# Preparing the second layer's weight sums in other pieces, on other engines and queues, while the first layer runs

## The chip, the cores and the metric

One core of a Trainium2 chip runs the whole kernel. TensorE (PE) multiplies matrices, with its weight loads recorded apart as PEld; VectorE (DVE), ScalarE (ACT) and GpSimd (POOL) do the element work, and SyncE (SP) issues DMAs and nothing else. ACT issues DMAs too. Every engine takes its instructions strictly in the order in which they were written, so an instruction that waits holds up all that stands behind it on its engine. The metric is the time of one execution on the device in microseconds: before the change the median of three runs is 1815.99 us (1813.62 to 1821.92).

## The reference

Three stages follow one another on 8 sequences of 576 tokens with 512 features.

```python
# 1: attention inside chunks of 64 tokens, 8 heads of 64
attn = softmax(q_c @ k_c^T / sqrt(64));  x = attn @ v_c
# 2: first layer
xn = (x - mean) / sqrt(var + 1e-6) * g_ln
x  = x + relu(xn @ w_ch1) @ w_ch2            # 512 -> 2048 -> 512
# 3: second layer, with its own weights
u   = x + (x^T @ U @ V)^T                     # U 576x32, V 32x576: mixes tokens
out = u + relu(u @ w_ch1') @ w_ch2'           # 512 -> 2048 -> 512
```

The weights, U and V arrive as 64-bit floats, which the kernel takes as pairs of 32-bit words and converts itself.

## The kernel before

Every matmul runs on operands split into a high and a low part, three products for one. The 4608 tokens are 36 tiles of 128.

**First layer.** Twelve blocks of three tiles, 16 steps each, 192 steps in all. A step is `g1` (12 matmuls of 384 columns into `psh`), then ScalarE's relu (L659, high part) and VectorE's L660 (low part), and `g2` of the step two back (9 matmuls of 512 columns into `acc`). At the end of a block `finish` (L677) adds `acc` onto `x` on VectorE, three tiles, and the next block's accumulation can begin only then. All else is written in between: the attention of a later block (L361/362 transposes, small matmuls into `psm`, L460 to L479 softmax on VectorE, L469 exp on ScalarE, scattered to DRAM as `sp` by ScalarE's queue at L586 and gathered at L591, L485 transpose, L514 the scaled result), its layer norm (L520 to L544), another scatter and gather, and L596, L598, L599 on VectorE, ScalarE and GpSimd, which give the next block's input. `z_mm` and `z_out` (L622) form the rank-32 product for the low-rank term and put it out as `zd`.

**Weights of the second layer.** The second layer uses a seven-product (Strassen-like) scheme on 256-wide halves, so it wants block sums of its weights. They are made beside the first layer, in 16 units, the first weight's eight before the second's. A unit loads two raw pieces of 512 KB (ScalarE's queue, L174 or L176), scales the two words of each on ScalarE (L186, L187), joins them on VectorE in a burst of five instructions (L192, L193, L196, L197, L198: `pre_b`), forms four sums on GpSimd (L219 to L222, 128x256 each: `pre_s`), splits seven results in a high part (ScalarE's L231) and a low part (VectorE's L236), and stores each result (256 KB, ScalarE's queue, L241, `wd<-wsp`), through two output slots in turn. A step is cut into thirds, and `at3` puts every piece of unit u into third 160 + 22u + x, with x from a table; steps 53 to 173.

**Second layer.** Five superblocks of 7, 7, 8, 7, 7 tiles, 112 units of six matmuls each (448 or 512 columns). Its weights come back from `wd` by 560 loads of 256 KB on SP (`w_in`, L962) into a ring. At a superblock's end the results are transposed by VectorE (L946, into four buffers `zt`) and stored (L957, `out<-zt`, four DMAs a tile), while the next superblock's tokens are loaded from `x1d` (L770, four DMAs a tile), turned by VectorE (L777) and given the low-rank term: `zd` is loaded on all partitions (L631), summed on GpSimd (L635), rounded (L642, L643), multiplied (`pslow`) and added by VectorE (L805). All three loads and the stores share SP's queue. `l2_first` writes this for the first superblock into the last 16 steps of the first layer, from step e = 176.

```python
at(NF * (NB - 2) + 13, make_vst)                       # V converted in step 173
for u in range(2 * NPR):                               # block sums: u-th unit
    for x, fn, n in ((0, pre_load, 0), (9, pre_load, 1), (5, pre_a, 0), (8, pre_b, 0), ...
        at3(160 + 22 * u + x, fn, u, ...)
```

Of the kernel before, what the change touches and what calls it, by code (L numbers as in the profile page):

```python
# [18 lines left out]
def fused_kernel(ctx, tc, q, k, v, g_ln, w1_a, w2_a, U, V, w1_b, w2_b, out):  # L19
    nc = tc.nc  # L20
# [12 lines left out]
    SB = (7, 7, 8, 7, 7)  # L33
    NPR = NF // 2
# [38 lines left out]
    w_d = {(w, m, p): dr.tile([P, DM], F32, name=f"wd{w}_{m}_{p}") for w in range(2) for m in range(7) for p in range(NPR)}  # L73
# [95 lines left out]
    def pre_load(u, n):  # L169
        which, p = divmod(u, NPR)  # L170
        f = 2 * p + n
        raw = pre[u, n] = raw_tile()
        if which:
            nc.scalar.dma_start(out=raw.rearrange("p a w -> p (a w)"), in_=w2_b.bitcast(I32)[f * P:(f + 1) * P, :])  # L174
        else:
            nc.scalar.dma_start(  # L176
                out=raw.rearrange("p (k f) w -> p k (f w)", k=KT),
                in_=w1_b.bitcast(I32)[:, f * 2 * P:(f + 1) * 2 * P].rearrange("(p k) f -> p k f", k=KT),
            )

    def pre_words(u, n):
        return pre[u, n][:, :, 1], pre[u, n][:, :, 0]

    def pre_a(u, n):
        hw, lw = pre_words(u, n)
        nc.scalar.activation(out=hw.bitcast(F32), in_=hw.bitcast(F32), func=AF.Copy, scale=2.0 ** -112)  # L186
        nc.scalar.activation(out=lw.bitcast(F32), in_=lw.bitcast(U32), func=AF.Copy, scale=2.0 ** -52)  # L187

    def pre_b(u, n):
        e = pl["e"]  # L190
        hw, lw = pre_words(u, n)
        nc.vector.tensor_scalar(out=e.bitcast(I32), in0=hw, scalar1=0x0FFFFFFF, scalar2=3, op0=ALU.bitwise_and, op1=ALU.logical_shift_left)  # L192
        nc.vector.scalar_tensor_tensor(out=hw, in0=hw, scalar=-0x80000000, in1=e.bitcast(I32), op0=ALU.bitwise_and, op1=ALU.bitwise_or)  # L193

        hw, lw = (a.bitcast(F32) for a in (hw, lw))
        nc.vector.tensor_scalar(out=e.bitcast(I32), in0=hw.bitcast(I32), scalar1=-0x00800000, scalar2=None, op0=ALU.bitwise_and)  # L196
        nc.vector.tensor_tensor(out=lw, in0=lw, in1=e, op=ALU.mult)  # L197
        nc.vector.tensor_tensor(out=hw, in0=hw, in1=lw, op=ALU.add)  # L198

    def pre_blocks(u):  # L200
        which = u // NPR
        e, z = [], []
        for n in range(2):
            hw, lw = (a.bitcast(F32) for a in pre_words(u, n))
            if which == 0:
                v = hw.rearrange("p (t c) -> p t c", t=KT)
            else:
                v = hw.rearrange("p (c t) -> p t c", t=KT)
            e.append([v[:, 0:2], v[:, 2:4]])
            z += [lw[:, m * 256:(m + 1) * 256].rearrange("p (t c) -> p t c", t=2) for m in range(2)]  # L210
        (a11, a12), (a21, a22) = e
        if which:
            a12, a21 = a21, a12
        return a11, a12, a21, a22, z

    def pre_s(u):
        a11, a12, a21, a22, (s1, s2, s3, s4) = pre_blocks(u)
        tt = nc.gpsimd.tensor_tensor
        tt(out=s1, in0=a21, in1=a22, op=ALU.add)  # L219
        tt(out=s2, in0=s1, in1=a11, op=ALU.subtract)  # L220
# [12 lines left out]

    def pre_l(u, c):
        m, o, x = pre["c", c]
        nc.vector.tensor_tensor(out=o[:, 1], in0=x, in1=f32(o[:, 0]), op=ALU.subtract)  # L236

    def pre_d(u, c):
        which, p = divmod(u, NPR)
        m, o, x = pre["c", c]  # L240
        nc.scalar.dma_start(out=w_d[which, m, p], in_=f32(o).rearrange("p w t c -> p (w t c)"))  # L241
# [347 lines left out]
    def gather(key):  # L589
        w = t1.tile([P, 4, P], F32, tag="w" if key < 2 * NT else "cvd", name="w")  # L590
# [29 lines left out]
    def z_out(b):  # L620
        z4 = t1.tile([P, DM], F32, tag="xn" if b >= B - 2 else "cvd", name="z4")
# [61 lines left out]
    O = (0, 1, 5, 6, 4, 2, 3)  # L683
    UNITS = 2 * 7 * NPR
# [647 lines left out]
```

## Time and profile before

| quantity | value |
|---|---|
| median of three runs | 1815.99 us (1813.62 to 1821.92) |
| the profiled execution | 1820.96 us |
| its span | 1819.1 us |
| PE busy | 1672.3 us, 92% of the span |
| VectorE busy | 1156.7 us, 64% |
| ScalarE busy | 601.8 us, 33% |
| GpSimd busy | 353.4 us, 19% |
| mean granted TensorE clock | 0.969 |

The profiled execution is 5 us above the median and within the three runs. Times of rows count from the start of the span; the first layer's steps with block sums beside them run from about 330 to 936 us, its last 16 steps to 1030 us, the second layer after them. [...]

### The profile page before, as it was taken

The page shows a single profiled execution, that of the slowest core. Times are in us where ns is not written, and L with a number is a line of the kernel's source. Part 1 is how long each engine was busy: PE and PEld are TensorE (multiplying, and loading weights), DVE is VectorE, ACT ScalarE, POOL GpSimd, SP SyncE. Part 2 cuts the span into 40 slices and gives each one's busy share as a digit, 9 for nine tenths or more (in the row PEclk, how much of TensorE's full clock was granted, in tenths as well). Part 3 has the DMA queues.
Part 4 walks back from the last instruction along what each step waited for, and adds up shares of the span by engine and source line. Part 5 has one row for each costly group of instructions (what it writes and reads, how often), then busy time and mean ns, then how long its engine had stood idle before and what let it go on. Part 6 is the DMA issues. An engine that isn't in the chain of part 4 may idle for free.

```text
span 1819.1 us, 28472 instructions
## 1 busy us (share of the span) xinstructions
PE 1672.3 (92%) x9890; PEld 1454.7 (80%) x9890; DVE 1156.7 (64%) x2384; ACT 601.8 (33%) x1122; POOL 353.4 (19%) x355
## 2 busy tenths in 40 slices
PE   6899998989899999999989999989997999899995
PEld 5788887878788788778777898978986888799994
DVE  7887544564756667576644259638836963884774
ACT  5554211222222232233221233424432442344341
POOL 1000011212122122212130033132033205202410
PEclk8999999999999999999989999999998999899998
DMA  6443333556466574556424288778776766777772
GB/s 163 125 131 100 93 72 77 147 144 170 136 160 169 154 197 145 151 165 166 144 91 149 84 243 256 214 200 259 207 200 205 237 192 195 244 226 215 251 214 77
DMA packets 384431, 307.94 MB, mean 169 GB/s; under 512 B 196513, under 2 KB 277409, under 8 KB 384290
## 3 DMA queue, kind: packets, MB, share of 16 engines
q1 hardware_dynamic: 314602, 230.22, 45.7%
q10 hardware_dynamic: 69688, 75.92, 13.3%
q8 instruction: 79, 1.29, 0.3%
q14 instruction: 62, 0.51, 0.1%
HBM read 241.53 MB, written 64.49 MB: 168 GB/s over the span
## 4 chain that ended last, share of the span: by engine, by line
PE 42%; DMA 10%; DVE 5%; issue 3%; SPq 2%; POOL 2%; ACT 1%; ACTq 1%; DVEq 0%; POOLq 0%
PE ps L60 31%; PE acc L60 5%; PE psh L60 4%; DMA out<-zt 3%; DMA zr<-zd 3%; DMA wr<-wd 2%; SPq L957 1%; DMA xw<-x1d 1%; DMA sp<-xn 1%; DVE zt L946 1%; DMA w<-sp 1%; PE psm L60 0%; PE pslow L60 0%; POOL zr L635 0%; ACTq L586 0%
## 5 line engine op out<-in xcount | busy, mean ns | idle before, releaser
L60 PE MATMUL ps<-act,wr 128*128 128x448 f32 (+1 forms) x2100 | 465.0, 379 | 12.9 <-POOL act L833 5.6
L60 PEld LDWEIGHTS ps<-act,wr 128*128 128x128 f32 x2100 | 402.1, 193 | 62.5 <-POOL act L833 6.4
L60 PE MATMUL psh<-act,w0h 128*128 128x384 f32 x1536 | 407.2, 346 | 41.5 <-DVE act L660 20.1
L60 PE MATMUL acc<-w1h,act 128*128 128x512 f32 x1152 | 403.2, 404 | 12.6 <-ACT e L469 9.6
L60 PEld LDWEIGHTS psh<-act,w0h 128*128 128x128 f32 x1536 | 287.6, 193 | 69.8 <-DVE act L660 28.0
L60 PEld LDWEIGHTS acc<-w1h,act 128*128 128x128 f32 x1152 | 219.6, 191 | 65.9 <-ACT e L469 11.0
L60 PE MATMUL psh<-act,w0l 128*128 128x384 f32 x768 | 263.9, 344 | 0.9 <-DVE w0l L148 0.9
L660 DVE SCALAR_TENSOR_TENSOR act<-psh,act 128x384 fp32r<-128x384 f32 x192 | 106.1, 553 | 243.3 <-ACT act L659 243.1
L60 PE MATMUL acc<-w1l,act 128*128 128x512 f32 x576 | 229.7, 399 | 0.0
L659 ACT ACTIVATE act<-psh 128x384 fp32r<-128x384 f32 x192 | 93.9, 489 | 298.4 <-PE psh L60 198.2
L60 PEld LDWEIGHTS psh<-act,w0l 128*128 128x128 f32 x768 | 148.0, 193 | 1.2 <-DVE w0l L148 1.2
L60 PEld LDWEIGHTS acc<-w1l,act 128*128 128x128 f32 x576 | 110.1, 191 | 17.9
L231 ACT CAST wsp<-raw 128x256 fp32r<-128x256 f32 x112 | 53.7, 480 | 180.0 <-DMA wd<-wsp 42.0
L890 ACT ACTIVATE h<-h 128x448 f32<-128x448 f32 (+1 forms) x80 | 46.8, 591 | 143.2 <-DVE h L900 101.5
L524 POOL TENSOR_SCALAR rs<-mv 128x1 f32<-128x1 f32 x36 | 8.4, 234 | 432.0 <-DVE mv L522 424.2
L236 DVE TENSOR_TENSOR wsp<-raw,wsp 128x256 fp32r<-128x256 f32 x112 | 61.2, 547 | 29.6 <-ACT wsp L231 25.3
L599 POOL TENSOR_TENSOR act<-wT,act 128x512 fp32r<-128x512 f32 x27 | 34.8, 1287 | 195.8 <-ACT act L598 187.0
L896 DVE TENSOR_TENSOR h<-ps,h 128x448 f32<-128x448 f32 (+1 forms) x40 | 24.1, 626 | 70.2 <-PE ps L60 70.2
L635 POOL TENSOR_TENSOR zr<-zr 128x512 f32<-128x512 f32 x24 | 30.9, 1287 | 189.3 <-DMA zr<-zd 183.6
L883 POOL TENSOR_TENSOR h<-h,h 128x448 f32<-128x448 f32 (+1 forms) x40 | 52.5, 1330 | 42.8 <-DVE hr0l L870 21.5
L929 POOL TENSOR_TENSOR uq<-rs,uq 128x448 f32<-128x448 f32 (+1 forms) x9 | 11.8, 1334 | 189.2 <-DVE uq L923 145.9
L60 PE MATMUL ps<-hr0h,wr 128*128 128x448 f32 (+1 forms) x140 | 47.0, 375 | 0.3 <-issue 0.2
(222 smaller groups left out, 2558.2 us busy)
## 6 DMA issues: line engine op xcount, KB each, us to landing
wr<-wd SPq DMA_DIRECT2D x560, 256.0 KB
wd<-wsp ACTq DMA_DIRECT2D x112, 256.0 KB
raw<-in_moe_w_ch ACTq DMA_DIRECT2D x32, 512.0 KB
w<-sp ACTq DMA_DIRECT2D x54, 256.0 KB
x1d<-x SPq DMA_DIRECT2D x36, 256.0 KB
xw<-x1d SPq DMA_DIRECT2D x144, 64.0 KB
v_pl<-in_v SPq DMA_DIRECT2D x132, 64.0 KB
raw<-in_moe_w_ch SPq DMA_DIRECT2D x64, 128.0 KB
```

The source lines that it names most:

```text
L60: nc.tensor.matmul(o, lhsT=l, rhs=r, start=start, stop=stop, **kw)
L231: nc.scalar.copy(out=o[:, 0], in_=src[m])
L236: nc.vector.tensor_tensor(out=o[:, 1], in0=x, in1=f32(o[:, 0]), op=ALU.subtract)
L599: nc.gpsimd.tensor_tensor(out=lo, in0=x, in1=f32(hi), op=ALU.subtract)
L635: nc.gpsimd.tensor_tensor(out=zr[:, 0], in0=zr[:, 0], in1=zr[:, 1], op=ALU.add)
L659: nc.scalar.activation(out=hi, in_=ps, func=AF.Relu)
L660: nc.vector.scalar_tensor_tensor(out=lo, in0=ps, scalar=0.0, in1=f32(hi), op0=ALU.max, op1=ALU.subtract)
L883: nc.gpsimd.tensor_tensor(out=b11, in0=b12, in1=b11, op=ALU.subtract)
L890: relu = lambda a: nc.scalar.activation(out=a, in_=a, func=AF.Relu)
L896: vt(out=c12, in0=ps, in1=c12, op=ALU.add)
L946: nc.vector.transpose(out=z[:, a:a + m // 32, k_, :], in_=u_of(s, k_, h)[:, o:o + m].rearrange("p (a j) -> p a j", j=32),)
L957: eng.dma_start(out=out[r + 32 * a:r + 32 * a + 32, :].rearrange("j (g c) -> g j c", g=4), in_=z[:, a, :])
```

## The change

Line numbers of the changed kernel are 15 to 29 higher than those of the same line before; the rows of program order below have each kernel's own.

1. Block sums. There are 32 half units, the second weight's first. Raw loads go out on SP's queue. Each of ScalarE's and VectorE's instructions of `pre_a` and `pre_b` gets a third of its own by `place`, at most one per engine and third, none in a block's steps 15 and 0, with gaps between what depends on what (`PRE_GAPS`, in thirds). The sums move from GpSimd to VectorE (L221, two per third): 32 of 128x256 for the second weight, 64 of 128x128 for the first. The second weight's results are still split and stored one by one, with three output slots; the first weight's in batches of three and four (384 and 512 columns, 32 splits instead of 56). There are 88 stores instead of 112: 56 of 256 KB, 16 of 384 KB and 16 of 512 KB. The pieces lie in steps 56 to 177.
2. First layer. From block 6 on, the first tile's attention is written one step earlier, so its L485 leaves the block's finishing step for the one before; loads of q and k are spread over 7 to 10 steps instead of 4 to 8; gathers of scores, V's conversion and `z_out` use other buffers, and `z_out` and part of `z_mm` come one to five steps later.
3. First superblock. The loads and sums of `z` begin three steps later, `x1_load` and `x1_turn` are set out by a table instead of one a step, the low-rank products come two a step instead of four.
4. Second layer. The turning of each loaded tile is written 11 units behind its load instead of 8. A tile's four stores are cut by 32 partitions (32 x 4 x 128 in DRAM, 2 KB of each partition) and no longer by 128 columns (4 x 32 x 128, 512 B of each of 128 partitions). `w_d` is one DRAM tile per weight and piece; TensorE's instructions of the second layer are the same.

```diff
+    PRE_G, PRE_N = 168, (11, 22)
+    PRE_GAPS = (4, 1, 1, 1, 1, 1, 4, 1)
+    PRE_SKIP, PRE_CAP = (15, 0), {"POOL": 1}
...
-    def pre_s(u):
-        a11, a12, a21, a22, (s1, s2, s3, s4) = pre_blocks(u)
-        tt = nc.gpsimd.tensor_tensor
-        tt(out=s1, in0=a21, in1=a22, op=ALU.add)
...
+    def pre_s(u, n):
+        a11, a12, a21, a22, (s1, s2, s3, s4) = pre_blocks(u)
+        out, x, y, op = ((s1, a21, a22, ALU.add), (s2, s1, a11, ALU.subtract), (s3, a21, a11, ALU.subtract), (s4, a12, s2, ALU.subtract))[n]
+        nc.vector.tensor_tensor(out=out, in0=x, in1=y, op=op)
...
-        for a in range(4):
-            eng = nc.scalar if s == len(SB) - 1 and a % 2 else nc.sync
-            eng.dma_start(out=out[r + 32 * a:r + 32 * a + 32, :].rearrange("j (g c) -> g j c", g=4), in_=z[:, a, :])
+        for g in range(4):
+            eng = nc.scalar if s == len(SB) - 1 and g % 2 else nc.sync
+            eng.dma_start(out=out[r:r + P, g * P:(g + 1) * P].rearrange("(a j) c -> j a c", j=32), in_=z[32 * g:32 * g + 32])
...
-            at(e + 1 + t, x1_load, 0, t)
-            at(e + 2 + t, x1_turn, 0, t)
+            at(e + (0, 2, 2, 4, 5, 6, 7)[t], x1_load, 0, t)
+            at(e + (2, 4, 5, 6, 7, 8, 9)[t], x1_turn, 0, t)
...
-                    side(u + 8, x1_turn, (s + 1, t))
+                    side(u + 11, x1_turn, (s + 1, t))
...
-                    s = g + {3: (2, 5, 8), 4: (-1, 2, 5)}.get(n, (-2, 1, 5))[t]
-                    at(s - (1 if n < 5 else 2), st_A, i)
+                    s = g + {3: (2, 5, 8), 4: (-1, 2, 5), 5: (-2, 1, 5)}.get(n, (-3, 1, 5))[t]
+                    at(s - (1 if n < 5 or t == 0 else 2), st_A, i)
...
+        def place(x, eng, fn, *a):
+            while x // 3 % NF in PRE_SKIP or slots.get((x, eng), 0) >= PRE_CAP.get(eng, 1):
+                x += 1
+            slots[x, eng] = slots.get((x, eng), 0) + 1
+            at3(x, fn, *a)
+            return x
...
+        def conv5(u, x, first):
+            y = place(max(x - 9, free[u % 2] + g_free, 159), "SP", pre_load, u)
+            y = place(max(x, y + g_load), "ACT", pre_a, u, 0)
+            z = place(y + 1, "ACT", pre_a, u, 1)
+            y = place(max(y + g_act, first), "DVE", pre_b, u, 0)
+            for n in range(1, 5):
+                y = place(max(y + 1, z + g_act if n == 3 else 0), "DVE", pre_b, u, n)
+            return y
...
+        def parts(u, x, batch, slot):
+            y = place(max(x, out_at[slot] + g_out), "ACT", pre_hi, u, batch, slot)
+            y = place(y + g_lo, "DVE", pre_lo, u, batch, slot)
+            out_at[slot] = place(y + g_store, "SPA", pre_d, u, batch, slot)
+            return y
```

VectorE around the finish of a block, about 785 to 794 us of the trace. Before, with `raw` and `v_pl` the raw words and their scratch, `act` the relu's low part, `kt_pl`, `mx`, `e` the attention's, `x` the finish:

```order
L236 TENSOR_TENSOR wsp<-raw,wsp 128x256
L192 TENSOR_SCALAR v_pl<-raw 128x512
L193 SCALAR_TENSOR_TENSOR raw<-raw,v_pl 128x512
L196 TENSOR_SCALAR v_pl<-raw 128x512
L197 TENSOR_TENSOR raw<-raw,v_pl 128x512
L198 TENSOR_TENSOR raw<-raw 128x512
L660 SCALAR_TENSOR_TENSOR act<-psh,act 128x384
L485 STREAM_TRANSPOSE kt_pl<-w 128x4x4x32
L460 TENSOR_REDUCE mx<-psm 128x8 x2
L461 TENSOR_TENSOR mx<-mx 128x16
L465 TENSOR_TENSOR e<-psm,mx 128x256 x2
L677 TENSOR_TENSOR x<-acc,x 128x512 x3
```

The same place on VectorE in the changed kernel, where L678 is the relu's low part, L695 the finish, L221 the sums and L246 the low split:

```order
L678 SCALAR_TENSOR_TENSOR act<-psh,act 128x384
L503 STREAM_TRANSPOSE kt_pl<-w 128x4x4x32
L678 SCALAR_TENSOR_TENSOR act<-psh,act 128x384
L478 TENSOR_REDUCE mx<-psm 128x8 x2
L479 TENSOR_TENSOR mx<-mx 128x16
L483 TENSOR_TENSOR e<-psm,mx 128x256 x2
L695 TENSOR_TENSOR x<-acc,x 128x512 x3
L221 TENSOR_TENSOR raw<-raw 128x128 x2
L246 TENSOR_TENSOR wsq<-raw,wsq 128x3x128
L221 TENSOR_TENSOR raw<-raw 128x128 x2
L678 SCALAR_TENSOR_TENSOR act<-psh,act 128x384
```

The burst of five and the low split ahead of the relu's low part are gone, the transpose has moved ahead of the step, and four sums and a split of three results stand behind the finish.

VectorE where V is converted, in step 173 (about 938 to 948 us). Before, with `vst` the converted V and `wT` the last block's input:

```order
L105 TENSOR_SCALAR cvt<-cvt 128x288
L290 TENSOR_TENSOR vst<-cvt 32x288 x2
L236 TENSOR_TENSOR wsp<-raw,wsp 128x256
L660 SCALAR_TENSOR_TENSOR act<-psh,act 128x384
L596 STREAM_TRANSPOSE wT<-w 128x4x4x32
```

And in the changed kernel:

```order
L108 TENSOR_SCALAR cvt<-cvt 128x288
L308 TENSOR_TENSOR vst<-cvt 32x288 x2
L203 TENSOR_TENSOR raw<-raw,v_pl 128x512
L205 TENSOR_TENSOR raw<-raw 128x512
L678 SCALAR_TENSOR_TENSOR act<-psh,act 128x384
L221 TENSOR_TENSOR raw<-raw 128x128 x2
L614 STREAM_TRANSPOSE wT<-w 128x4x4x32
L246 TENSOR_TENSOR wsq<-raw,wsq 128x3x128
```

The conversion itself stays where it was; two joins of raw words stand ahead of the relu's low part in place of one split, and two sums ahead of the transpose.

SP's queue at the start of the second superblock, before:

```order
L962 DMA wr_9730<-wd_6_0_172 128x512
L962 DMA wr_9765<-wd_6_1_173 128x512
L957 DMA out<-zt 4x32x128 x4
L962 DMA wr_9767<-wd_6_2_174 128x512
L631 DMA zr<-zd_240 128x1x512
```

And in the changed kernel:

```order
L989 DMA wr_9535<-wd_0_124 128x512
L989 DMA wr_9572<-wd_1_125 128x512
L984 DMA out<-zt 32x4x128 x4
L989 DMA wr_9574<-wd_2_126 128x512
L649 DMA zr<-zd_144 128x1x512
```

The stores keep their place among the weight loads and the loads of `z`; only their form differs.

## Rows read from the trace of the kernel before

**Rows 1.** The page: its span, and each engine's busy time and instructions.

```profile
span 1819.1 us, 28472 instructions
PE 1672.3 (92%) x9890; PEld 1454.7 (80%) x9890; DVE 1156.7 (64%) x2384; ACT 601.8 (33%) x1122; POOL 353.4 (19%) x355
```

**Rows 2.** Busy time by stretch: length, PE, PEld, DVE, ACT, POOL, PEclk, DMA.

```profile
330.00:936.00 606.00, 561.53 (x3965) 481.75 (x3964) 381.97 (x781) 168.71 (x344) 139.00 (x157) 0.98 0.56 156
936.00:1030.00 94.00, 81.76 (x378) 69.88 (x377) 34.71 (x86) 16.13 (x32) 8.92 (x7) 0.95 0.30 98
1176.00:1246.00 70.00, 58.88 (x270) 51.95 (x269) 31.31 (x83) 19.63 (x38) 27.68 (x24) 0.95 0.74 209
1360.00:1410.00 50.00, 40.03 (x161) 32.23 (x160) 31.38 (x79) 12.83 (x22) 19.13 (x15) 0.90 0.68 200
1525.00:1578.00 53.00, 43.46 (x181) 37.20 (x180) 32.68 (x85) 14.17 (x27) 17.53 (x16) 0.87 0.74 225
...
1803.00:1818.00 15.00, 0.00 (x0) 0.00 (x0) 0.90 (x5) 0.00 (x0) 0.00 (x0) 0.50 0.25 73
```

**Rows 3.** What PE waited for, 330 to 936 us: total, times, longest.

```profile
PE psh L60 <- DVE act L660: 12.9, 10, 4.4
PE acc L60 <- ACT e L469: 9.6, 5, 3.0
PE psh L60 <- ACT act L598: 5.8, 5, 3.0
PE zps L60 <- ACT z L622: 4.0, 1, 4.0
```

**Rows 4.** Timeline, 785 to 793 us: start, duration, engine, line; idle before and releaser.

```profile
787.43 0.69 DVE L198 TENSOR_TENSOR raw<-raw 128x512 f32<-128x512 f32 x1
...
788.16 0.70 ACT L231 CAST wsp<-raw 128x256 fp32r<-128x256 f32 x1 [3.94 <-DVE raw L198]
...
792.01 1.88 DVE L677 TENSOR_TENSOR x<-acc,x 128x512 f32<-128x512 f32 x3
...
792.84 0.77 PE L60 MATMUL acc<-w1h,act 128*128 128x512 f32 x1 [2.82 <-ACT e L469]
```

**Rows 5.** The chain of waits, 721 to 731 us: start, duration, what.

```profile
721.53 1.13 POOL raw L219
...
725.08 1.09 POOL raw L222
726.17 1.24 POOL xn L544
```

**Rows 6.** Costliest groups by shape: busy, mean ns, idle before and what ended it.

```profile
L236 DVE TENSOR_TENSOR wsp<-raw,wsp 128x256 fp32r<-128x256 f32 x112 | 61.2, 547 | 29.6 <-ACT wsp L231 25.3 <-issue 3.8 <-DMA q<-in_q 0.2
L514 DVE TENSOR_TENSOR x<-psm,sm 128x256 f32<-128x256 f32 x66 | 24.5, 413 | 7.5 <-DMA x1d<-x 4.9 <-PE psm L60 2.4
L193 DVE SCALAR_TENSOR_TENSOR raw<-raw,v_pl 128x512 int32<-128x512 int32 x32 | 23.2, 724 | 1.1
L219 POOL TENSOR_TENSOR raw<-raw 128x256 f32<-128x256 f32 x16 | 16.3, 1020 | 105.4 <-DVE raw L198 105.4
```

**Rows 7.** Timeline of VectorE and GpSimd, 510 to 513 us.

```profile
510.58 1.41 POOL L544 TENSOR_TENSOR xn<-xn,gbc 128x512 f32<-128x512 f32 x1 [0.66 <-DVE xn L543]
510.88 1.67 DVE L193 SCALAR_TENSOR_TENSOR raw<-raw,v_pl 128x512 int32<-128x512 int32 x1
```

**Rows 8.** Timeline of ScalarE and PE, 940 to 946 us.

```profile
943.73 0.49 ACT L659 ACTIVATE act<-psh 128x384 fp32r<-128x384 f32 x1 [2.69 <-DVE wsp L236]
946.13 0.69 PE L60 MATMUL psh<-act,w0h 128*128 128x384 f32 x1 [5.33 <-ACT act L598]
```

**Rows 9.** The chain of waits at the second layer's starts.

```profile
977.03 4.72 DMA xw<-x1d
...
1391.70 6.29 DMA out<-zt
```

**Rows 10.** What PE and VectorE waited for, 1030 to 1800 us.

```profile
PE pslow L60 <- DVE ux L805: 10.0, 2, 6.4
...
DVE zt L946 <- DMA out<-zt: 48.8, 16, 7.6
```

**Rows 11.** SP's queue, 1208 to 1215 us and at the end: start, issue time.

```profile
1208.34 2.39 SPq L957 DMA_DIRECT2D out<-zt  x4
...
1212.76 1.85 SPq L770 DMA_DIRECT2D xw<-x1d  x4
...
1803.26 8.72 SPq L957 DMA_DIRECT2D out<-ux  x8
```

More of the change, by code (lines that the diff above doesn't have):

```diff
@@ L167, in fused_kernel, with pre_load @@
     pre = {}
[L169 to L172, printed above, removed]
+    def pre_load(u):
+        pp, half = divmod(u, 2)
+        which, p = divmod(pp, NPR)
+        if ("raw", u % 2) not in pre:
+            pre["raw", u % 2] = raw_tile()
+        raw = pre["raw", u % 2]
         if which:
-            nc.scalar.dma_start(out=raw.rearrange("p a w -> p (a w)"), in_=w2_b.bitcast(I32)[f * P:(f + 1) * P, :])
+            nc.sync.dma_start(out=raw.rearrange("p a w -> p (a w)"), in_=w2_b.bitcast(I32)[(2 * p + half) * P:(2 * p + half + 1) * P, :])
@@ L175, in pre_load @@
         else:
[L176 to L182, printed above, removed]
+            src = w1_b.bitcast(I32)[:, 4 * p * P:4 * (p + 1) * P].rearrange("(p m t) f -> p m t f", m=2, t=2)
+            nc.sync.dma_start(out=raw.rearrange("p (m c) w -> p m (c w)", m=2), in_=src[:, :, half])
@@ L189, in pre_b @@
     def pre_b(u, n):
         e = pl["e"]
[L191 to L196, printed above, removed]
@@ L234, in pre_l @@
[L234 to L241, printed above, removed]
+            fw, lw = (a.bitcast(F32) for a in pre_words(n))
+            v.append(fw.rearrange("p (c h t) -> p h t c", h=2, t=2))
+            s += [lw.rearrange("p (s t c) -> p s t c", s=2, t=2)[:, m] for m in range(2)]
@@ L1163, in fused_kernel @@
                 runs = len(list(chunk_runs(2 * TPB * (n + 1), 2 * TPB)))
[L1164 removed]
+                first, last = {2: (13, 16), 3: (8, 12), 4: (4, 9)}.get(n, (3, 9) if runs == 1 else (0, 9))
+                parts_ = last + 1 - first
                 for part in range(parts_):
[L1166 removed]
+                    at(g + first + part, load_qk, n + 1, part, parts_)
         for n in range(NB):
@@ new lines, in fused_kernel, with sums @@
+        out_at = [0] * 5
+        def sums(u, y):
+            at_ = []
+            for n in (0, 2):
+                y = place(y, "DVE", pre_s, u, n)
+                at3(y, pre_s, u, n + 1)
+                at_.append(y)
+                y += 1
+            return at_
+        def parts(u, x, batch, slot):
[3 more added lines that the diff above has]
+            return y
@@ new lines, in fused_kernel @@
+        x = PRE_G
+        slot = 0
+        for u in range(2 * NPR, 4 * NPR, 2):
+            y = conv5(u, x, 0)
+            for n in range(2):
+                z = parts(u, y + g_hi + n, n, slot % 3)
+                slot += 1
+            y = conv5(u + 1, x + 5, y + 1)
+            y = sums(u, y + 1)
+            for n in range(5):
+                z = parts(u, (y[0], y[0], y[1], y[1], y[1])[n] + g_pool, 2 + n, slot % 3)
+                free[n > 1] = max(z, y[1])
+                slot += 1
+            x += PRE_N[1]
```

159 lines of the change are left out of this document (98 added, 61 removed).

## The prediction, made before the changed kernel ran

> **What bounds the kernel now.** I read the page first. PE is busy 1672.3 of 1819.1 us [rows 1], so at most 147 us of the span can go while its work stays as it is, and TensorE's instructions are not changed. The question is where those 147 us lie and which of them the changed work holds. The windows by stage say it [rows 2]. In the stretch with block sums, 330 to 936 us, PE is idle 606 - 561.5 = 44.5 us, and the clock is granted at 0.98, which is another 0.02 x 606 = 12 us. In the first layer's last steps, 936 to 1030, it is idle 94 - 81.8 = 12.2 us, and the clock costs 0.05 x 94 = 4.7. At three starts of superblocks it is idle 11.1, 10.0 and 9.5 us, together 30.7, and the clock of 0.95, 0.90 and 0.87 costs 3.5 + 5.0 + 6.9 = 15.4. At the end there are 15 us in which PE does nothing at all. These four places hold 44.5 + 12.2 + 30.7 + 15 = 102 us of idle time and 32 of slow clock.
>
> Next, the waits in the first stretch [rows 3]. PE waits there for VectorE's L660 (12.9 us, up to 4.4 at a time), for ScalarE's exp L469 (9.6), for the next block's input at L598 (5.8) and once for the low-rank product (4.0). None of these names the block sums; that they stand behind is seen only in the timeline. At 787.4 the fifth instruction of a burst (L198) runs, ScalarE's split L231 has waited 3.94 us for it, and the relu queued behind that split is late by as much; the finish L677 begins at 792.01 and PE's next `acc` matmul has lost 2.82 us [rows 4]. The row puts that wait down to L469, but L469 was itself late behind L465, which stood behind the burst. The 4.0 us for the low-rank product are of the same kind: four sums on GpSimd hold its queue from 721.5 to 726.2, and the layer norm's L544 can begin only then [rows 5].
>
> **The change part by part.**
>
> *Burst, splits and sums in the first layer (a).* Placing each instruction alone takes the burst away from the finish and from the transposes. I count as held by the old placing the whole 12.9 us behind L660, two thirds of the 9.6 behind L469 (the rest I leave to the attention's own scatter and gather), and the 4.0 of the low-rank product, since no sum runs on GpSimd any more: 12.9 + 6.4 + 4.0 = 23.3 us. The 5.8 at L598 stay, with the other 15 us.
>
> Against this stands more work on VectorE. The trace has no such sum there. The nearest row for 256 columns is L514 with 413 ns [rows 6]; for 128 columns I take 0.3 us, between half of that and all of it (0.21 to 0.41). That is 32 x 0.413 + 64 x 0.3 = 13.2 + 19.2 = 32.4 us (27 to 39). The low splits become 88 instead of 112; by the 413 ns, 56 of 256 columns would go for 16 of 384 and 16 of 512, so 56 x 0.413 = 23.1 us for 16 x (0.62 + 0.83) = 23.2: nothing but per-instruction overhead is saved, and for that and for less disturbance by GpSimd I take 5 us. VectorE is up by 27 us, from 382 to 409 of 606 us, 67%. Spread over a block, these 27 us cost nothing where PE's step has room for them; five of sixteen steps behind a block's start carry most of the attention on VectorE, so I let 27 x 5 / 16 = 8 us through to PE. If all room were gone it is 27, if none is needed 0. Then 23.3 - 8.4 = 15 us of idle time go net, and with a third of the idle time a third of the clock's 12 us: 4. Term (a): -19 us, from -31 (23.3 and 8 of clock) to +8.
>
> ScalarE gets 24 stores and 24 splits fewer, and the raw loads leave its queue; it is busy 169 of 606 us and I cost that at nothing. The raw loads now stand in SP's queue among loads of q, k and v. What covers them is the gap of at least four thirds of a step between load and first use; a load that comes later than that holds ScalarE's scaling, and the relu behind it.
>
> VectorE's two-input instructions get slower when GpSimd runs: L193 took 1.67 us beside L544's 1.41, against a mean of 724 ns [rows 6, 7]. [...]
>
> *End of the first layer (b).* The largest wait, 5.33 us at 946, stays: ScalarE and VectorE convert V there in one piece, and the relu at 943.73 comes behind [rows 8]. In the changed order two joins of raw words stand ahead of VectorE's relu in place of a split and a store; that is worth -1 to +1. Of the remaining 12.2 - 5.3 = 6.9 us I expect half to go, since the first tokens' loads are set apart in SP's queue: one of them, 4.72 us, is on the chain [rows 9]. With 1.5 of clock that is -5 us, from -8 to +2. What is late next is the low-rank product, two a step instead of four.
>
> *Starts of superblocks (c).* VectorE waits 48.8 us in 16 waits for `out<-zt` to leave its four buffers, and PE 10.0 us for the low-rank result behind it [rows 10]. A store of the old form takes 2.39 us to issue in four and 6.29 us to land; the loads `xw<-x1d`, which already have the new form, 1.85 and 4.72 [rows 9, 11]. A tile so gains 0.5 + 1.6 = 2.1 us; seven tiles at three starts are 44 us, of which no more than the 30.7 of idle time can be given back, and much lies beside the weights' loads, which share the queue. The turn written three units later costs up to three units; a unit is a 112th of a superblock, and the span holds 560 in about 780 us, so 1.4 us each: 4 us per start, 12 in all, where the token load had landed long before. I take a third of 30.7 + 15.4 = 46: -16 us, from -31 to +12.
>
> *The last stores (d).* In the last 15 us the DMA share is 0.25 and 73 GB/s [rows 2]: a quarter of the engines works. Eight stores take 8.72 us to issue [rows 11]; at the new form's 1.85 / 4 it is 3.7, so 5.0 less, and the landing 1.6 to 4 less. I take -8, from -11 to 0.
>
> [...]
>
> Sum: -19 - 5 - 16 - 8 = -48 us. The profiled execution took 1820.96 us, so 1773; it stands 5.0 above the median of 1815.99, so the median to expect is **1768 us**. Its own range is 1745 to 1790: half of each term's distance to its ends, not all in one direction.
>
> **The rivals.**
>
> 1. The first layer's waits belong to the attention (scatter to DRAM, gather, transposes), and the block sums only happen to stand there. For it: L469 and L598 are named in the waits, not the sums. Against: rows 4 and 5. Then (a) is +8, the rest stays: -21, so 1795.
> 2. VectorE becomes the bound behind each block's start: attention, split and four sums between finish and relu, as the order shows. The place is the five steps after a boundary; the price is the longest present wait of 4.4 us and about 2 of slow clock behind it in each of seven blocks, +45 instead of -19. With (b) to (d) that is +45 - 29 = +16: 1832, slower. It decides from 4.1 us per block on. Against: VectorE at 67%.
> 3. The later turn and the spread low-rank products cost what the stores give: (c) +12, (d) -2 with (a) and (b) as above: -14, 1802.
> 4. Stores of 32 partitions are slower. The trace has only loads in this form, and those are quicker [rows 11]. If landing doubles from 6.29, seven tiles at three starts lose what they now wait, 30 us in all, and the end 6: -24 + 36 = +12, 1828. [...] No run here shows a store of that kind.
> 5. The raw loads come late on SP, so that ScalarE waits as it did: (a) shrinks to about -5, giving 1782, inside the range above.
>
> **How the numbers follow.** Forecast 0.55, rival 1 0.17, rival 2 0.08, rival 3 0.11, rival 4 0.04, rival 5 0.05. Half a per cent, 9 us, is about what a measurement of this kernel can tell from no change. Faster (below 1807): forecast 0.53, rival 1 0.14, rival 3 0.07, rival 5 0.05, so 0.79. Slower (above 1825): 0.07 + 0.03 from rivals 2 and 4, 0.10. Same: 0.11. The range is 1738 to 1813; it takes in rivals 1, 3 and 5, and leaves out rivals 2 and 4 and some unexpected gain.
>
> **What would show it.** Term (a): between the end of the first weights and about 936 us, PE idle near 30 instead of 44.5, its waits for the relu's low part mostly gone, none for the low-rank product. If instead PE's waits for the relu's low part grow behind each finish and VectorE has no idle time there, rival 2. Term (b): the wait near 946 still there, about 5 us. Term (c): waits of `zt` for `out` down from 48.8 us to under 20, idle time at each start under 8. Term (d): DMA share well over 0.25 after the last matmul, and some 8 us less from it to the end; if the stores land later than 6 us each, rival 4. The forecast is wrong if (a) gives nothing: then VectorE's 27 us have cost as much as the burst.

## The result, and the profile after

The changed kernel takes 1758.17 us (median of 4 runs, 1754.48 to 1762.89) against 1814.8 us before, taken beside it (4 runs); the ratio is 0.9688, interval 0.9645 to 0.9732. Forecast were 1768 us, 1738 to 1813. A second set of four (`after_again`) gave 0.9679 (0.9646 to 0.9712). The profiled execution took 1754.48 us.

The page of the changed kernel, span and busy times:

```profile
span 1752.7 us, 28378 instructions
PE 1660.1 (95%) x9890; PEld 1448.8 (83%) x9890; DVE 1186.0 (68%) x2456; ACT 599.2 (34%) x1098; POOL 300.3 (17%) x291
```

The span is 66.4 us shorter. VectorE is 29 us busier and GpSimd 53 us less, as the moved sums would have it, and PE's share is up by 3 points. The stages of [rows 2], by the same places of the program, in the changed kernel (columns as there; PEclk is the granted clock as a share of the full one, DMA the mean busy share of the core's 16 DMA engines):

```profile
326.00:910.00 584.00, 558.59 (x3966) 483.14 (x3965) 411.65 (x857) 170.35 (x325) 85.90 (x92) 0.98 0.59 160
910.00:996.00 86.00, 79.59 (x375) 68.58 (x374) 34.11 (x83) 14.37 (x28) 10.29 (x8) 0.94 0.39 121
...
1142.00:1214.00 72.00, 63.70 (x300) 56.11 (x299) 36.61 (x89) 22.55 (x43) 28.97 (x25) 0.98 0.83 233
1326.00:1376.00 50.00, 47.34 (x211) 38.20 (x210) 41.08 (x98) 17.11 (x29) 22.94 (x18) 1.00 0.80 224
1484.00:1530.00 46.00, 38.83 (x176) 33.86 (x175) 35.63 (x91) 15.30 (x29) 19.28 (x17) 0.93 0.88 264
...
1746.00:1752.00 6.00, 0.00 (x0) 0.00 (x0) 0.70 (x5) 0.00 (x0) 0.00 (x0) 0.60 0.64 175
```

In the stretch with block sums PE is idle 25.4 us instead of 44.5; at the three starts 8.3 + 2.7 + 7.2 = 18.2 instead of 30.7, and the clock there costs 1.4 + 0 + 3.2 = 5 us instead of 15; after the last matmul the DMA share is 0.64 instead of 0.25. Cut at the same matmuls, the two traces divide the 66.4 us like this (steps are counted from 0, and each cut is the step's first matmul; step 175 begins at 936.5 us before and at 910.0 after, the border of [rows 2]):

| stretch | before | after | difference | forecast |
|---|---|---|---|---|
| start to step 53 | 319.1 | 315.0 | -4.1 | 0 |
| steps 53 to 175 (a) | 617.3 | 595.0 | -22.3 | -19 |
| steps 175 to 191 (b) | 89.9 | 82.6 | -7.2 | -5 |
| step 191 and the second layer (c) | 771.7 | 751.8 | -19.9 | -16 |
| after the last matmul (d) | 21.1 | 8.2 | -12.8 | -8 |

The first line is no effect: step 53 began between 314.3 and 320.4 us in the other runs of nearly the same beginning. The median to median gain, 57 us, is smaller for the same reason: this profile was taken of a short execution, and that of before of a long one. One pair of traces is good to some microseconds a stretch: steps 53 to 175 took 610.6 us in `b_store`, which has the kernel before unchanged there, and 598.9 and 592.2 in `after_again` and `a_oldstore`, which have the changed kernel there. So (a) lies between 12 and 25 us.

What PE waits for in the changed kernel, 315 to 880 us, to be read beside [rows 3]:

```profile
PE psm L63 <- DVE kt_pl L380: 12.9, 7, 3.0
PE psh L63 <- DVE act L678: 8.1, 4, 2.8
PE psm L63 <- DMA v_pl<-in_v: 4.2, 2, 2.4
```

The waits behind the finish, for the next block's input and for the low-rank product are gone, and the longest is 3.0 instead of 4.4 us. In all, PE's listed waits are 25.2 us instead of 44.4. Before, a second wait at the finish belonged to them:

```profile
PE acc L60 <- DVE x L677: 3.0, 1, 3.0
```

But a new one has come up that the prediction doesn't have: seven times, once a block, the first tile's scores wait for the transpose of k (L380). One of them, 747 to 755 us of the changed kernel (VectorE, GpSimd and PE):

```profile
750.11 1.66 POOL L562 TENSOR_TENSOR xn<-xn,gbc 128x512 f32<-128x512 f32 x1 [1.37 <-DVE xn L561]
750.67 1.65 DVE L205 TENSOR_TENSOR raw<-raw 128x512 f32<-128x512 f32 x1
752.25 0.54 DVE L678 SCALAR_TENSOR_TENSOR act<-psh,act 128x384 fp32r<-128x384 f32 x1
...
752.71 0.60 DVE L221 TENSOR_TENSOR raw<-raw 128x128 f32<-128x128 f32 x2
...
753.86 0.67 DVE L380 STREAM_TRANSPOSE kt_pl<-k 128x512 f32<-128x512 f32 x1
...
754.67 1.13 PE L63 MATMUL psm<-kt_pl,qt 64*64 64x64 f32 x32 [3.02 <-DVE kt_pl L380]
```

VectorE has no gap here: a piece of the block sums in each third, one of them (L205) taking 1.65 us while GpSimd's L562 runs, where its median is 0.69, and the transposes stand behind them, written only one step ahead of the matmuls that want them.

The 8.1 us for L678 are four waits, at 423.9, 512.0, 592.7 and 670.8 us, and in each ScalarE's scaling L190 ahead of the relu had waited 3.6 to 5.1 us for a raw load on SP's queue. That of 592.7, from SP's queue to PE:

```profile
578.38 8.57 SPq L335 DMA_DIRECT2D k<-in_k  x10
587.06 0.41 SPq L179 DMA_DIRECT2D raw<-in_moe_w_ch  x1
```

```profile
590.99 0.65 ACT L190 ACTIVATE raw<-raw 128x512 f32<-128x512 f32 x1 [4.23 <-DMA raw<-in_moe_w_ch]
591.55 0.47 ACT L677 ACTIVATE act<-psh 128x384 fp32r<-128x384 f32 x1
...
592.05 0.56 DVE L678 SCALAR_TENSOR_TENSOR act<-psh,act 128x384 fp32r<-128x384 f32 x1 [2.65 <-ACT act L677]
...
592.67 0.62 PE L63 MATMUL psh<-act,w0h 128*128 128x384 f32 x2 [2.79 <-DVE act L678]
```

Ten loads of k take SP's queue 8.57 us to issue, the raw load of the block sums stands behind them, ScalarE's scaling waits 4.23 us for it, and the relu waits behind the scaling. At 512.0 and 670.8 the load stands behind 13 and 10 such loads as well; at 423.9 only two stand right ahead of it. So none of these four is a burst of VectorE any more.

### The profile page after: what moved, and what is told of

It reads as the page before. It is cut to its first block, busy times and chain, and to the rows that moved or that the text cites. A ratio compares the mean times of both kernels' runs of the same rounds, so it can differ in the third digit from the quotient of the medians.

```text
span 1752.7 us, 28378 instructions
## 1 busy us (share of the span) xinstructions
PE 1660.1 (95%) x9890; PEld 1448.8 (83%) x9890; DVE 1186.0 (68%) x2456; ACT 599.2 (34%) x1098; POOL 300.3 (17%) x291
## 4 chain that ended last, share of the span: by engine, by line
PE 52%; DMA 9%; DVE 7%; SPq 3%; issue 2%; ACT 1%; ACTq 1%; POOL 0%; DVEq 0%; POOLq 0%
PE ps L63 37%; PE acc L63 7%; PE psh L63 7%; DMA q<-in_q 2%; SPq L335 2%; DMA raw<-in_moe_w_ch 1%; DMA w<-sp 1%; DMA k<-in_k 1%; DMA zr<-zd 1%; DMA v_pl<-in_v 1%; DMA out<-zt 1%; DMA sp<-xn 1%; PE psm L63 1%; DVE act L678 1%; DMA wr<-wd 0%
## 5 line engine op out<-in xcount | busy, mean ns | idle before, releaser
L63 PE MATMUL ps<-act,wr 128*128 128x448 f32 (+1 forms) x2100 | 458.1, 375 | 9.3 <-DVE h L927 3.6
L63 PEld LDWEIGHTS ps<-act,wr 128*128 128x128 f32 x2100 | 395.0, 190 | 58.5 <-DVE h L927 4.9
L63 PE MATMUL psh<-act,w0h 128*128 128x384 f32 x1536 | 401.1, 342 | 18.6 <-DVE act L678 11.8
L678 DVE SCALAR_TENSOR_TENSOR act<-psh,act 128x384 fp32r<-128x384 f32 x192 | 106.7, 556 | 233.2 <-ACT act L677 232.6
L190 ACT ACTIVATE raw<-raw 128x512 f32<-128x512 f32 x64 | 42.0, 670 | 83.6 <-DMA raw<-in_moe_w_ch 38.4
L653 POOL TENSOR_TENSOR zr<-zr 128x512 f32<-128x512 f32 x24 | 31.4, 1308 | 159.7 <-DMA zr<-zd 143.5
L562 POOL TENSOR_TENSOR xn<-xn,gbc 128x512 f32<-128x512 f32 x27 | 38.5, 1424 | 66.1 <-DVE xn L561 66.1
L63 PE MATMUL ps<-hr5h,wr 128*128 128x448 f32 (+1 forms) x140 | 46.5, 371 | 0.0
## 6 DMA issues: line engine op xcount, KB each, us to landing
raw<-in_moe_w_ch SPq DMA_DIRECT2D x48, 512.0 KB
```

What stands on the lines that cost most here:

```text
L63: nc.tensor.matmul(o, lhsT=l, rhs=r, start=start, stop=stop, **kw)
L190: nc.scalar.activation(out=w.bitcast(F32), in_=w.bitcast((F32, U32)[n]), func=AF.Copy, scale=2.0 ** (-112, -52)[n])
L562: nc.gpsimd.tensor_tensor(out=xn, in0=xn, in1=gbc, op=ALU.mult)
L653: nc.gpsimd.tensor_tensor(out=zr[:, 0], in0=zr[:, 0], in1=zr[:, 1], op=ALU.add)
L678: nc.vector.scalar_tensor_tensor(out=lo, in0=ps, scalar=0.0, in1=f32(hi), op0=ALU.max, op1=ALU.subtract)
```

## The experiments

Each kernel's ratio is to the kernel before on its own chip, where that took 1814.81 us for `b_store`, `a_oldstore`, `a_burst` and `a_pool`, 1806.3 for `a_noskip`, `a_attn`, `a_lead2` and `b_vst`, and 1816.13 for the rest, so kernels of different groups are compared by ratio.

**Only the stores.** `b_store` is the kernel before with the new form of the stores, `a_oldstore` the changed kernel with the old.

```diff
-        for a in range(4):
-            eng.dma_start(out=out[r + 32 * a:r + 32 * a + 32, :].rearrange("j (g c) -> g j c", g=4), in_=z[:, a, :])
+        for g in range(4):
+            eng.dma_start(out=out[r:r + P, g * P:(g + 1) * P].rearrange("(a j) c -> j a c", j=32), in_=z[32 * g:32 * g + 32])
```

> The kernel before with only the last part of the change: a tile's four stores cut by 32 partitions. Theory (stores of the old form hold VectorE's four buffers and the end of the kernel): the time after the last matmul falls from 21 us to about 8, the waits of VectorE for out<-zt in the second layer from 48.8 us to about 30, and the three starts give back 10 to 20 us of idle time and clock, so about -25 to -32 us: 1784 to 1790. Rival (the starts were eased by the later turning and the other order of z, the stores matter at the end alone): -12 us, 1803. Rival (stores out of 32 partitions are slow): no gain or a loss.

> The changed kernel with the old form of the stores. Theory: the mirror of the former, +25 to +32 us: 1783 to 1790, the 13 us of the end among them. Rival (the stores matter at the end alone): +13 us, 1771, with the starts of superblocks as in the changed kernel.

Measured: `b_store` 1785.43 us, ratio 0.9831 (0.9799 to 0.9863); `a_oldstore` 1790.2 us, 0.9868 (0.9820 to 0.9917). VectorE's waits for the stores in the second layer, with the new form in the kernel before (first fence) and with the old form in the changed kernel (second):

```profile
DVE zt L946 <- DMA out<-zt: 28.4, 14, 7.3
```

```profile
DVE zt L973 <- DMA out<-zt: 57.5, 15, 7.9
```

And the stretches after the last matmul, where in the first kernel the last eight stores of a queue are issued in 3.87 us and in the second the DMA share is a quarter again:

```profile
1776.99 3.87 SPq L957 DMA_DIRECT2D out<-ux  x8
```

```profile
1764.00:1779.00 15.00, 0.00 (x0) 0.00 (x0) 1.58 (x7) 0.00 (x0) 0.00 (x0) 0.50 0.26 76
```

From the second layer's first matmul to its last it is 767.5 us before, 750.4 in `b_store`, 764.2 in `a_oldstore`, 747.7 after; from there to the end 21.1, 7.8, 21.0 and 8.2. So the form of the stores alone is 13 us at the end and 13 to 17 in the second layer (`b_vst`, whose second layer is that of the kernel before, took 763.7), half of the whole gain. In the changed kernel itself VectorE's waits for the stores are as long as in `b_store`:

```profile
DVE zt L973 <- DMA out<-zt: 31.4, 14, 5.9
```

The two rivals (the end alone; slow stores) fall.

**The burst.** `a_burst`: the five joins of a half unit in one third again, which now waits until both words are scaled.

```diff
-            y = place(max(y + g_act, first), "DVE", pre_b, u, 0)
+            y = place(max(y + g_act, z + g_act, first), "DVE", pre_b, u, 0)
             for n in range(1, 5):
-                y = place(max(y + 1, z + g_act if n == 3 else 0), "DVE", pre_b, u, n)
+                at3(y, pre_b, u, n)
```

> The changed kernel with the five instructions that join the raw words written in one third again (3 us at a stretch on VectorE), everything else placed as in the changed kernel. Theory (the burst is what held the relu's low part and the finish): PE's waits in the stretch with block sums rise by 8 to 20 us, the waits for L678 above all, and the time to 1767 to 1780. Rival (what counts is only that nothing stands in steps 15 and 0, or that GpSimd's sums are gone): within 4 us of the changed kernel's 1758.

Measured: 1772.97 us, 0.9762 (0.9721 to 0.9802), 15 us over the changed kernel. The stretch 315 to 900 us of the changed kernel, and then of this one:

```profile
315.00:900.00 585.00, 559.59 (x4001) 484.08 (x3999) 410.03 (x853) 167.39 (x318) 87.47 (x95) 0.98 0.59 160
```

```profile
315.00:900.00 585.00, 551.77 (x3929) 475.99 (x3928) 406.07 (x846) 162.18 (x312) 79.85 (x90) 0.97 0.58 159
```

PE's idle time is 33.2 us instead of 25.4. What PE waited for in that stretch, the longest kind and the one that the expectation names:

```profile
PE psm L63 <- issue: 9.8, 4, 3.1
...
PE psh L63 <- DVE act L678: 5.9, 4, 4.3
```

The time came as expected, but not by the waits for L678, which are 5.9 us and not more than the changed kernel's 8.1. One of them, the longest, shows the way from a burst to PE that the prediction had:

```profile
423.54 1.67 DVE L199 SCALAR_TENSOR_TENSOR raw<-raw,v_pl 128x512 int32<-128x512 int32 x1
...
426.42 0.69 DVE L205 TENSOR_TENSOR raw<-raw 128x512 f32<-128x512 f32 x1
...
427.15 0.65 ACT L242 CAST wsq<-raw 128x256 fp32r<-128x256 f32 x1 [5.93 <-DVE raw L205]
...
428.22 0.56 DVE L678 SCALAR_TENSOR_TENSOR act<-psh,act 128x384 fp32r<-128x384 f32 x1 [1.10 <-ACT act L677]
428.83 1.01 PE L63 MATMUL psh<-act,w0h 128*128 128x384 f32 x2 [4.27 <-DVE act L678]
```

The split on ScalarE waits 5.93 us for the burst, the relu stands behind that split, its low part behind the relu, and PE behind that: the same path as in [rows 4]. Another burst reaches PE by another way:

```profile
571.89 0.69 DVE L205 TENSOR_TENSOR raw<-raw 128x512 f32<-128x512 f32 x1
...
574.02 1.01 PE L63 MATMUL psm<-v_pl,kt_pl 64*64 64x64 f32 x32 [3.08 <-issue]
```

Behind the burst, from 572.5 us on, VectorE reads the attention's `psm` (L478 to L483), and PE's next matmuls into `psm` have lost 3.08 us. The profile names no releaser for them, and of the four waits of this kind only this one has a burst right ahead, so this way is likely and not shown. No `acc` wait came back, and none was to be expected from bursts that stay out of steps 15 and 0.

**The sums.** `a_pool`: the 96 sums on GpSimd at the same places.

```diff
-        nc.vector.tensor_tensor(out=out, in0=x, in1=y, op=op)
+        nc.gpsimd.tensor_tensor(out=out, in0=x, in1=y, op=op)
```

> The changed kernel with the 96 sums on GpSimd in place of VectorE, at the same places. Theory by the prediction's term (VectorE's 32 us of sums let 8 us through to PE): VectorE's busy time in the stretch falls by about 30 us, and PE would gain 8 us by that, but sums of about 1 us each hold the layer norm's L562 and the splits behind them, so between -4 and +12 us: 1754 to 1770. Rival (the sums on GpSimd were the main cause of the waits before): +15 us or more.

Measured: 1753.97 us, 0.9656 (0.9624 to 0.9687), not to be told from the changed kernel. The same stretch:

```profile
315.00:900.00 585.00, 560.90 (x4032) 485.05 (x4031) 380.59 (x766) 166.72 (x318) 150.91 (x183) 0.98 0.59 161
```

VectorE has 29 us less to do and PE gains 1.3 of it. The waits for L380 stay at 12.8 us, and none for the low-rank product appears though the sums stand on GpSimd again. The engine of the sums mattered for neither.

**The steps kept free, and the attention's move.** `a_noskip` empties the skip list, `a_attn` puts the first tile's attention of blocks 6 to 11 back, `a_both` does both.

```diff
-    PRE_SKIP, PRE_CAP = (15, 0), {"POOL": 1}
+    PRE_SKIP, PRE_CAP = (), {"POOL": 1}
```

```diff
-... 5: (-2, 1, 5)}.get(n, (-3, 1, 5))[t]
-                    at(s - (1 if n < 5 or t == 0 else 2), st_A, i)
+... 5: (-2, 1, 5)}.get(n, (-2, 1, 5))[t]
+                    at(s - (1 if n < 5 else 2), st_A, i)
```

> The changed kernel with the pieces of the block sums allowed in a block's steps 15 and 0 as well (the skip list empty), the rest placed by the same rule. Theory A (the finish's waits, 9.6 and 3.0 us of `acc` before, went because those two steps are kept free): PE's waits of `acc` behind the finish come back with 6 to 12 us, 1764 to 1772. Theory B (they went because the first tile's attention is written a step earlier): no `acc` wait, and the time within 4 us of the changed kernel's 1758, as the pieces have 16 steps of a block instead of 14.

> The changed kernel with the first tile's attention of blocks 6 to 11 written where it was before (its transpose L503 in the finishing step again). Theory A: within 3 us of 1758, no `acc` wait. Theory B: the `acc` waits come back with 6 to 12 us, 1764 to 1772; the seven waits for L380, 12.9 us in the changed kernel, would go with the lead that this tile's transposes have again.

> The changed kernel with both at once: pieces of the block sums allowed in steps 15 and 0, and the first tile's attention in the finishing step again. Each alone brought no wait of `acc`. Theory (either one keeps VectorE free ahead of the finish, so that only both together show what it is worth): the waits of `acc` behind the finish come back with 5 to 10 us, and the kernel is slower than with either alone by about as much. Rival (the `acc` waits went with the bursts alone): `acc` waits under 2 us, time as with either alone, a ratio of about 0.965.

Measured: `a_noskip` 0.9653 (0.9621 to 0.9684), `a_attn` 0.9666 (0.9633 to 0.9700), `a_both` 0.9707 (0.9662 to 0.9753); the changed kernel beside the last, 0.9679. Theory A fails in `a_noskip`, which has no `acc` wait, and theory B in `a_attn`, which has one of 1.9 us instead of 6 to 12: undoing either alone costs nothing. What PE waited for (the `acc` waits, and for `a_noskip` those for L380), in `a_noskip`, `a_attn` and `a_both` in turn:

```profile
PE psm L63 <- DVE kt_pl L380: 6.7, 5, 2.2
```

```profile
PE acc L63 <- ACT e L487: 1.9, 1, 1.9
```

```profile
PE acc L63 <- ACT e L487: 7.1, 6, 2.3
```

The `acc` waits return in number only where both are undone, six of up to 2.3 us. Either the free steps or the earlier attention is enough to have VectorE ready for the finish; having both is paid for, since 14 steps must hold what 16 could and L380 waits 12.9 instead of 6.7 us. The stretch 315 to 900 us of `a_noskip`:

```profile
315.00:900.00 585.00, 570.67 (x4072) 495.44 (x4071) 422.90 (x883) 174.19 (x330) 86.53 (x95) 0.99 0.59 165
```

PE is idle 14.3 us there, 18.3 in `a_attn` and 25.0 in `a_both`, against 25.4 in the changed kernel. So keeping the two steps free, once the attention was moved, saved no idle time in these traces but cost 11 us of it. The times of the three overlap; the waits are clear, the worth in microseconds is not.

**The transposes.** `a_lead2` writes L379 and L380 of the first tile one step earlier; `a_lead2_noskip` empties the skip list too.

```diff
-                    at(s - (1 if n < 5 or t == 0 else 2), st_A, i)
+                    at(s - (1 if n < 5 else 2), st_A, i)
```

> The changed kernel with the first tile's transposes of q and k (L379, L380) written one step earlier than there, two steps ahead of their matmuls instead of one, for blocks 6 to 11. Theory (PE's seven waits for L380 are VectorE's queue of that one step, behind pieces of the block sums and one that GpSimd's L562 holds up): most of the 12.9 us go, and 8 to 12 us of the time: 1746 to 1750. Rival (the same queue holds the relu's low part in that step anyway, so the wait moves to L678): within 3 us of 1758.

> The changed kernel with both of what helped alone: the first tile's transposes of q and k one step earlier, and the pieces allowed in all 16 steps of a block. Theory (they relieve the same queue of VectorE in the same step, one by moving the transposes, the other by thinning the pieces): not the sum of their gains but little more than the better one, a ratio of 0.958 to 0.963. Rival (independent): 0.954 to 0.958.

Measured: `a_lead2` 0.9627 (0.9593 to 0.9661); `a_lead2_noskip` 1743.83 us, 0.9611 (0.9577 to 0.9644), against 1756.87 us of the changed kernel beside it. The stretch 315 to 900 us of the two:

```profile
315.00:900.00 585.00, 568.77 (x4059) 490.90 (x4058) 411.91 (x872) 171.54 (x328) 85.71 (x94) 0.99 0.60 163
```

```profile
315.00:900.00 585.00, 570.68 (x4074) 494.34 (x4072) 420.35 (x884) 173.88 (x330) 84.59 (x95) 0.99 0.60 165
```

PE's idle time is 16.2 and 14.3 us, against 25.4 in the changed kernel; `a_lead2` has no wait for L380 left. The second step adds little, as the first theory said: the intervals of the two overlap, and that of `a_noskip` alone overlaps both. `a_lead2_noskip` has the lowest ratio of all, about 13 us under the changed kernel beside it.

**The conversion of V.** `b_vst` is the kernel before, with the conversion at the head of step 173, ahead of the gather.

```diff
-        at(NF * (NB - 2) + 13, make_vst)
+        plan.setdefault(NF * (NB - 2) + 13, []).insert(0, (make_vst, ()))
```

> The kernel before with the conversion of V written at the start of step 173, ahead of the gather of scores, which stood ahead of it on ScalarE. Theory (the wait of 5.3 us at 946 was not the conversion's length but its late start behind a split that waited for a store and a gather that waited for a scatter, 4 us in all): the wait falls to about 3 or 4 us, since the gather's own wait stands behind the conversion now. Rival (the conversion's 7 us on both engines are the wait): 5 us stay, or more.

Measured in a single run: 1801.64 us against 1806.3 (1800.7 to 1811.75), which decides nothing; the trace does. ScalarE ahead of the conversion (L88) in the kernel before:

```profile
933.77 0.42 ACT L231 CAST wsp<-raw 128x256 fp32r<-128x256 f32 x1 [2.17 <-DMA wd<-wsp]
935.47 0.34 ACTq L591 DMA_DIRECT2D w<-sp  x1
935.86 0.46 ACT L88 ACTIVATE cvt<-vraw 128x288 f32<-128x288 f32 x1 [1.67 <-DMA sp<-xn]
```

What PE then waited for at that place in `b_vst`:

```profile
PE psh L60 <- ACT act L598: 1.9, 1, 1.9
```

It was 5.33 us [rows 8], and 3 or 4 were expected. The stretch of steps 175 to 191 in `b_vst`:

```profile
929.00:1011.00 82.00, 74.27 (x356) 63.73 (x355) 30.90 (x77) 12.77 (x25) 8.96 (x7) 0.98 0.34 113
```

That is 82.4 us from matmul to matmul, where the kernel before takes 89.9, `b_store` 90.6 and the changed kernel 82.6: this one edit gives as much there as the whole change, by one execution of each. PE's idle time there is 7.7 us instead of 12.2 (6.4 in the changed kernel); the rest goes with the granted clock, 0.98 in this execution where it was 0.95 [rows 2]. The conversion is as long as it was; what cost was that it began 4.7 us after the relu ahead of it (931.12), behind a split that waited for a store's slot and a gather that waited for its scatter. In the changed kernel it begins 0.8 us after the relu and the relu that follows comes right behind it, not behind a split's store:

```profile
903.92 0.49 ACT L677 ACTIVATE act<-psh 128x384 fp32r<-128x384 f32 x1 [2.35 <-PE psh L63]
...
904.73 0.46 ACT L91 ACTIVATE cvt<-vraw 128x288 f32<-128x288 f32 x1 [0.32 <-issue]
...
909.85 0.48 ACT L677 ACTIVATE act<-psh 128x384 fp32r<-128x384 f32 x1
```

**The later turn.** `a_turn8` turns the loaded tiles 8 units behind their loads again.

```diff
-                    side(u + 11, x1_turn, (s + 1, t))
-                    turned.append(u + 11)
+                    side(u + 8, x1_turn, (s + 1, t))
+                    turned.append(u + 8)
```

> The changed kernel with each loaded tile turned 8 units behind its load as before, not 11 (the low-rank products and additions follow it). Theory (the new stores made the waits at the starts short, the later turn is worth little): within 4 us of the changed kernel, the second layer's 748 us up to 752. Rival of the prediction (a later turn costs up to 4 us per start, 12 in all): faster by 5 to 12 us. Other rival (the later turn keeps VectorE from waiting for loads): slower by 5 to 10.

> The changed kernel once more, as the measure for the three runs beside it on the same chip. Expected ratio to the kernel before 0.965 to 0.973.

Measured: `a_turn8` 0.9675 (0.9647 to 0.9704), `after_again` 0.9679; from the second layer's first matmul to its last 747.8 and 746.8 us. The three units are worth nothing that can be measured either way.

## Why the prediction was right, and where its steps failed

**The whole** came out in direction and nearly in size: 57 us of median against 48.

**(a), -22 against -19** (-12 to -25 by the other traces), is right in sum and wrong in its parts. That a burst on VectorE costs PE time is shown: putting it back costs 15 us (`a_burst`). The path that I gave it (it holds a split, the split the relu, the relu PE) is there, at 428.8 us, but in `a_burst` most of the loss has other names. The waits for the relu's low part only fell from 12.9 to 8.1: those behind bursts are gone, and the four that stand there now come from the raw loads, which the prediction had as its fifth rival. Those at the finish, 9.6 and 3.0, went wholly, where I gave two thirds of the one. Those for the next block's input, 5.8, went where I said they stay; in `a_lead2`, without the waits for L380, 2.6 us of them stand again from 315 to 900 us, so in part they were only hidden. The price of VectorE's new work was too high: VectorE was busier by 29.7 us in the stretch (381.97 to 411.65), near my 27, but it let 1.3 through to PE (`a_pool`), not 8. One sum took 677 ns for 256 columns and 337 for 128, not the 413 and 300 that I took from L514; the same rows have L236, of the same shape, at 547. An average load of 70% (411.65 of 584 us) said more here than my five full steps of sixteen. In place of it came what I had not looked for, 12.9 us for L380. It is not the sums (`a_pool`) but a transpose written with one step's lead (`a_lead2`) in a queue that the two free steps had made denser (`a_noskip`). The term for the low-rank product was right by accident: 4.0 us went, but not because the sums left GpSimd, since with them there it didn't return. Which of the other edits freed it, `z_mm`'s later place, the sums' wider spacing or the other buffer of `z_out`, stays open.

**(b), -7.2 against -5**, is near in sum by two errors against each other. The step that failed is "the largest wait, 5.33 us at 946, stays: ScalarE and VectorE convert V there in one piece". I took the length of the conversion for the cause and counted only what stands between its end and the relu. `b_vst` shows that its late start was the larger part: the wait fell to 1.9 us. The half of the other 6.9 us and the 1.5 of clock that I expected from the first tokens' loads did not come: beside `b_vst` the changed kernel has only 1.3 us less idle time there, and its clock in the last steps is 0.94 where it was 0.95. PE waits there for the low-rank product, as I had said of what would be late next:

```profile
PE pslow L63 <- DVE uq L832: 4.5, 2, 4.3
```

**(c), -19.9 against -16, and (d), -12.8 against -8.** The mechanism held, and the stores alone account for most of it (13 to 17 and 13 us). But the waits for `zt` fell to 31.4 us and not under 20, and one start is idle 8.3 us and not under 8. In (d) the issue went from 8.72 to 3.76 us, as I had it (3.7), and from its end to the end of the kernel it is 2.9 us instead of 7.1: 4.3 less, a little more than my 1.6 to 4. What I left out is ahead of the issue: from the last matmul to the first of these stores it was 5.2 us and is 1.6, since VectorE's last transposes had waited for an earlier store to leave `zt`. The chain's last full piece of `out<-zt` shows it, before (first fence) and after:

```profile
1792.39 5.26 DMA out<-zt
```

```profile
1737.99 2.04 DMA out<-zt
```

The share of 0.25 is a mean over the 16 engines; which of them worked, and why no more, no row shows. The term's low end of -11 is worked out from no row either, and the measured 12.8 lies beyond it. In (c) the later turn costs nothing where I allowed 12.

**The range.** The forecast's own range, 1745 to 1790, does not follow from half of each term's distance to its ends, which gives 1751 to 1803; the measured 1758 lies in both.

**The rivals.** The first (attention alone) falls by `a_burst`, where the attention stays as it is in the changed kernel and the time rises. The second (VectorE the bound, slower) falls: PE's waits didn't grow behind the finishes, and 29 us more or less on VectorE can't be told. The third falls by (c), which is -19.9 and not +12, and for the later turn by `a_turn8`; the spread low-rank products were not run alone. The fourth falls by `b_store`: with stores out of 32 partitions the last eight of a queue are issued there in 3.87 us instead of 8.72 [rows 11], and VectorE's waits for `out<-zt` are 28.4 us instead of 48.8 [rows 10]; in the changed kernel the share after the last matmul rose from 0.25 to 0.64. The doubled landing that the rival takes is shown by no run: the longest piece of `out<-zt` on the chain is 5.36 us in `b_store` where it was 6.29 [rows 9]. The fifth is there beside the forecast: raw loads late on SP's queue are all 8.1 us of PE's waits for L678. I read that from the trace; a kernel with these loads on another queue wasn't run.

## What to carry to other kernels

Read a stall's cause from the engine's queue ahead of the late instruction, not from the name the wait carries: in this kernel a 3 us burst showed up as a wait for a relu, and a conversion that began late looked like a conversion that is long. When background work is spread out one piece at a time, look next for foreground pieces with a lead of a single step, since these now wait behind it, and ask of every step kept free what it does to the others. And look at the DMA share in a stretch where nothing but DMAs run: here a share of 0.25 rose to 0.64 with the form of the stores, and that form was worth half of the gain.

## What the runs showed of the hardware

That an engine keeps to the written order is shown for VectorE where an order and times stand side by side (784.7 to 794 and 941 to 946 us before, 771 to 783 and 910 to 916 after), and that a waiting instruction holds up what stands behind it by the split of `a_burst` that waits 5.93 us with the relu behind it.

Beside GpSimd's multiplication in the layer norm some of VectorE's instructions took longer, before as after: L193 1.67 us [rows 7] where its median is 0.69, and L205 of the changed kernel 1.65 us where its median is 0.69. These have two inputs, but it is not two inputs that the traces tell apart, since before the change L192 with one, whose median is 0.42 us, took 1.52 at 605.4 us beside L544. Still, with the 96 sums on GpSimd the ratio was 0.9656, with them on VectorE 0.9688, less apart than can be measured. And the last stores of the kernel, the same bytes in DMAs of the same 64 KB, went out at a share of 0.25 as 4 x 32 x 128 in DRAM out of 128 partitions and at 0.64 as 32 x 4 x 128 out of 32. In the middle of that stretch, without its ends, the share was 0.27 before (1804 to 1816 us) and this after:

```profile
1747.00:1751.00 4.00, 0.00 (x0) 0.00 (x0) 0.00 (x0) 0.00 (x0) 0.00 (x0) 0.52 0.93 254
```
